# Row maximum of the softmax over the state subtracted by GpSimd in five of eight batches, with another order of operations

## The chip, the cores and the metric

The kernel runs on one core of a Trainium2 chip. Its time is the device time of one execution in microseconds (us); times of several executions are given as a median. Engines are called TensorE (PE in the profile), VectorE (DVE), ScalarE (ACT), GpSimd (POOL) and SyncE (SP, which only issues transfers here).

## The reference, cut to what matters

Two stages. The first is an attention between x (8 batches, 8 heads, 512 rows, 64 columns) and a state (8, 8, 32 rows, 64 columns), with a softmax in each direction. The second runs over the 544 rows of both results, 512 columns wide (all heads), with a convolution of three rows between two products.

```python
def _attn_ref(x, state):                      # x: 8,8,512,64   state: 8,8,32,64
    scores = scale * np.matmul(x, state.transpose(0, 1, 3, 2))
    scores = scores - scores.max(-1, keepdims=True)      # over the 32 rows of the state
    a = np.exp(scores)
    a /= a.sum(-1, keepdims=True) + 1e-09
    xread = np.matmul(a, state)
    scores2 = scale * np.matmul(state, x.transpose(0, 1, 3, 2))
    ...                                                  # the same softmax, over the 512 rows of x
    return np.concatenate([xread, np.matmul(a2, x)], axis=2)

def _moe_ref(x, w_in, conv_w, w_out):         # x: 8,544,512   w_in: 512,1024   w_out: 1024,512
    h = np.maximum(x @ w_in, 0.0)
    conv_out = ...                            # conv_w[0]*row before + conv_w[1]*row + conv_w[2]*row after
    gate = 1.0 / (1.0 + np.exp(-conv_out))
    return h * gate @ w_out
```

## The kernel before

Nothing is looped at run time: the program is one straight list of 1,673 operations, made in a fixed numbering and then put out in the order that the string ORDER gives. Each engine runs its own operations in that order, and waits only where data or a buffer asks for it. A number in ORDER is an operation; a negative number -n puts n blocks of filler products on TensorE; a `v` behind a number runs an operation that is ScalarE's on VectorE. BANKS gives, in the same order, which of eight PSUM banks each result takes. Transfers are issued from SyncE's queue in the list's order too, so a load that waits for a free buffer holds those behind it.

For each batch b the steps are these.

- `xt_load`, `x_load`: x is loaded twice, transposed (tag `xt`, four buffers) and plain (tag `xx`).
- `scores` (TensorE) and `keep_scores`: the scores of both directions, kept in a buffer `at` of 128x1024.
- `top`, `exp2`, `norm2`, then `flip` or `turn`, `read`, `divide`, `read_flip`: the softmax over x and its product, for the 32 state rows.
- `softmax(b)`, for batches 1 to 7: the softmax over the 32 rows of the state, in ten operations on a buffer `af` of 128x1024, of which there is one. `att_flip` (L477, VectorE) transposes blocks of 32, `att_top` (L481, VectorE) takes the maximum of each 32, `att_sub` (L484) subtracts it, `att_exp` (L487, ScalarE), `att_sum` (L491, VectorE), `att_norm`, `att_div` (L498), `att_back` (L501), all VectorE, then the split into a rounded part and a rest, `att_high` (ScalarE) and `att_low` (VectorE). Batch 0 has a softmax of its own in halves.
- `state_product(b, hf)` (L588): the state times a half of w_in, so that the read of x and its product with w_in become one product; the result is split into two parts as well (`state_high`, `state_low`). Its two buffers have the tags `u0` and `u1`, two buffers each, or those that ELSEWHERE names.
- `hidden`, for steps i = 8 b + f with f from 0 to 7: six products (L677) from the split scores and the split state product, then `relu` (L216, ScalarE mostly), `join` and `edge` (L695: copies of one element per partition, on ScalarE for batches 0 to 2 and on GpSimd from batch 3), `middle`, two taps `before` (L720) and `behind` (L725), `sigmoid` (L729), `gate` (L734), the split `gate_high` (L221) and `gate_low` (L224), and twelve products `project` (L752) with w_out.

Weights are loaded in pieces and rounded by ScalarE and VectorE (`w_abs` to `w_sign`) at the start. Every large product from batch 1 on is made three times, with the high and low parts (PASSES). The 64 rows of both sides at the ends of the batches go through the smaller operations `side_...` and `tail`.

Of the kernel before, what the change touches and what calls it, by code (L numbers as in the profile page):

```python
# [13 lines left out]
ALU = mybir.AluOpType  # L14
# [37 lines left out]
ELSEWHERE = {(B - 1, 0): "xt", (B - 1, 1): "xt", (B - 2, 1): "at"}  # L52
# [12 lines left out]
01234567012342147536047260413756043175231253540504646457065407654075647040601324576723015145145720  # L65
1364527301037010143640171657632323420232402476371654207654120721740521640450740156052404370334063
# [3 lines left out]
99 0 -1 122 -5 -7 -1 -1 -1 -1 -1 -1 -1 100 102 121 1 125 127v 21 101 126 103 104 22 24 128 143 144 151 129 23 25 15 17  # L70
# [3 lines left out]
208 541 159 55 137 138 526 500 209 517 502 479 480 528v 481 56 210 163 164 165 211 63 65 213 529 569 570 518 242 599  # L74
# [35 lines left out]
1567 1129 1124 1557 1565 1130 1568 1133 1163 1134v 1137v 1125 1569 1148 1164 1167 379 1131v 1570 1149 1152 1138 1135  # L110
1139 1140 1165 1168 1153 422 1141 380 381 382 417 1150 1571 1178 1142 1166 1136 383 1154 1143 1179 1572 1238 1182 1169
1155 1156 420 421 1574 418 419 1193 1194 1157 416 1208 1196 1170 1195 1171 1239 1241 1181 1223 1146 425 1197v 426 1172
1158 1183 1261 1306 1209 1210 1180 1211 423 1151 424 1224 1198 1291 1184 1185 1145 1160 1147 1186 1240 1262 1199 1161
1265v 1173 1263 1200 1201 1187 1144 1188 1266 1267 1212 1264 1268 1213 1214 1321 1269 1575 1307 1202 1576 1308 1322
1324 1226 1323 1175 1227v 1159 1174 1162 1177 1215 1216 1176 1203 1573 1228 1577 1578 1242 1243 1579 1225 1229 1244
1192 1230 1231 1207 1190 1217 1205 1232 1245 1246 1276 1325 1126 1191 1206 1189 1277 1204 1292 1366 1218 1580 1294
1219 458 459 1221 1582 1583 1278 1279 1367 1369 1233 1247 1248 1310 1311 1222 1295 1309 1584 1585 1586 1236 1270 1220
1370 1251 1257v 460 1293 463 465 1271 464 1280 1258 468 1234 466 1587 1296 1297 1237 1252 1312 461 1235 1298 1259 1260
1588 1313 1368 1595 1249 1281 1253 462 1326 1581 1299 1389 1273 1282 1283 1284 1285 1596 1254 1351 1352 1390v 1391
1250 1300 1392 1314 1589 1255 1275 1336 1371 1337 469 1327 1132 1286 1301 1597 1598 1274 1289 1599 1272 1419 1434 1288  # L120
1303 1315 1316 1340 1339 1328 1329 1330 1318 1420 1423 1590 1593 1592 1393v 1331 1304 1290 1305 1600 1355v 1356 1422
1353 1338 1372 467 1479 1357 1404 1341 1342 1358 1601 1394 1333 1373 1374 1343 1344 1603 1287 1302 1317 1435 1405 1407
1436 1602 1604 1605 1606 1332 1359 1320 1360 1361 1607 1608 1421 1408v 1609 1335 1319 1424 1464 1406 1425 1345 1375
1395 1396 1449 1346 1350 1376 1611 1348 1334 1349 1364 1347 1362 1612 1613 1409 1363 1438v 1437 1410 1411 1377 1614
# [48 lines left out]
def fused_kernel(ctx: ExitStack, tc: tile.TileContext, xT, xn, stT, w_in, conv_w, w_out, out):  # L173
# [62 lines left out]
    add = plan.add  # L236
# [229 lines left out]
    def rows(b):  # L466
        return af[b].rearrange("p (k n) -> p k n", n=NS)
# [4 lines left out]
    def per_row(t):  # L472
        return t.unsqueeze(2).broadcast_to([P, KT, NS])
# [9 lines left out]
    def att_sub(b):  # L483
        V.tensor_tensor(rows(b), rows(b), per_row(s1.pop(b)), op=ALU.subtract)  # L484
# [529 lines left out]
```

## Time and profile before

| | |
|---|---|
| median of 2 executions | 354.12 us (354.07 to 354.16) |
| the profiled execution | 353.49 us |
| its span, first to last instruction | 351.7 us |
| TensorE, VectorE, ScalarE, GpSimd busy | 344.9, 317.1, 255.1, 29.0 us |
| products on TensorE (as recorded) | 2505 |
| bytes moved | 39.24 MB |

The span is what the trace covers; the time of an execution has about 1.8 us around it. The views show times from the span's start.

### The profile page before, as it was taken

Reading aid. Unit: us, or ns where it says so; the run is one execution under the profiler, and the core shown is the slowest. Engines: PE = TensorE matmul, PEld = TensorE weight load, DVE = VectorE, ACT = ScalarE, POOL = GpSimd, SP = SyncE. Lnnn points to the kernel's source line nnn. Section 1 sums busy time; section 2 is a strip of 40 time slices with the busy share of each in tenths; the row PEclk is TensorE's granted clock in tenths of the full one; section 3 lists DMA queues with packets and bytes.
Section 4 is the critical chain, followed back from the end, with each engine's and each line's share of the span. In section 5 each row is a group of like instructions: output and inputs, shape, how many; then the busy total and the mean of one; then the engine's idle time right before and its main releaser. Section 6 shows DMA issues by size and latency. Waiting matters only on the chain.

```text
span 351.7 us, 6630 instructions
## 1 busy us (share of the span) xinstructions
PE 344.9 (98%) x2505; PEld 269.0 (76%) x2505; DVE 317.1 (90%) x545; ACT 255.1 (73%) x554; POOL 29.0 (8%) x90
## 2 busy tenths in 40 slices
PE   8998999999999999999999999999999999999995
PEld 5765767788688877887788878886887678888884
DVE  1999999999999999999999999989997898899870
ACT  2998999998778888786975677647766865564462
POOL 1000000000000000030110112000411101122000
PEclk9999999999999999999999999999999999999999
DMA  7999988323730255152110010010000021001024
GB/s 237 389 337 361 331 292 332 123 66 104 253 121 0 69 174 178 63 178 79 43 60 2 0 60 33 30 60 32 2 2 0 30 91 31 22 3 37 0 89 149
DMA packets 19343, 39.24 MB, mean 112 GB/s; under 512 B 1904, under 2 KB 8176, under 8 KB 19312
## 3 DMA queue, kind: packets, MB, share of 16 engines
q1 hardware_dynamic: 18880, 38.54, 31.6%
q8 instruction: 19, 0.31, 0.4%
q10 hardware_dynamic: 432, 0.29, 0.3%
q14 instruction: 12, 0.10, 0.1%
HBM read 27.81 MB, written 11.01 MB: 110 GB/s over the span
## 4 chain that ended last, share of the span: by engine, by line
PE 95%; DMA 3%; DVE 1%; issue 0%; ACT 0%
PE acc L752 47%; PE ps_h L677 22%; PE ps_hs L662 4%; PE ps_u L595 4%; PE acc_t L752 3%; DMA xt<-xT 3%; PE ps_h L684 3%; PE ps_r L401 2%; PE ps_s L325 2%; PE idle L233 2%; PE acc_c L752 2%; PE acc L766 2%; PE ps_t L372 1%; PE ps_x L542 1%; PE ps_f L414 0%; DVE nm L354 0%
## 5 line engine op out<-in xcount | busy, mean ns | idle before, releaser
L752 PE MATMUL acc<-wo,g 128*128 128x512 f32 x723 | 175.6, 393 | 0.0
L752 PEld LDWEIGHTS acc<-wo,g 128*128 128x128 f32 x723 | 134.6, 188 | 29.3 <-issue 1.3
L677 PE MATMUL ps_h<-a,u 128*128 128x512 f32 x336 | 82.8, 392 | 0.1
L677 PEld LDWEIGHTS ps_h<-a,u 128*128 128x128 f32 x336 | 62.5, 188 | 14.1 <-ACT u L221 0.8
L729 ACT ACTIVATE t<-t 128x512 f32<-128x512 f32 x64 | 40.0, 630 | 19.5 <-DVE t L725 19.4
L725 DVE SCALAR_TENSOR_TENSOR t<-h,cw,t 128x512 f32<-128x512 f32 (+1 forms) x64 | 47.0, 745 | 0.7
L720 DVE SCALAR_TENSOR_TENSOR t<-h,cw,t 128x511 f32<-128x511 f32 x64 | 46.9, 744 | 0.4 <-ACT t L210 0.3
L221 ACT ACTIVATE g<-t 128x512 fp32r<-128x512 f32 (+1 forms) x62 | 38.3, 621 | 12.3 <-DVE t L734 8.8
L734 DVE SCALAR_TENSOR_TENSOR t<-t,h 128x512 f32<-128x512 f32 (+1 forms) x64 | 42.2, 668 | 4.1 <-ACT t L729 4.0
L224 DVE TENSOR_TENSOR g<-t,g 128x512 fp32r<-128x512 f32 (+1 forms) x62 | 41.2, 673 | 3.4 <-ACT g L221 3.3
L216 ACT ACTIVATE h<-ps_h 128x512 f32<-128x512 f32 x59 | 34.8, 599 | 11.7 <-PE ps_h L677 8.3
L210 ACT ACTIVATE t<-h,cw 128x512 f32<-128x512 f32 x53 | 38.0, 725 | 0.7 <-DVE g L224 0.5
L695 POOL COPY h<-hs 128x1 f32<-128x1 f32 x40 | 15.3, 400 | 136.7 <-DVE t L734 111.8
L772 ACT ACTIVATE o<-acc 128x512 f32<-128x512 f32 (+1 forms) x30 | 16.2, 554 | 10.8 <-PE acc L752 7.4
L695 POOL COPY hs<-h 128x1 f32<-128x1 f32 x40 | 13.3, 349 | 83.9 <-ACT h L216 69.8
L224 DVE TENSOR_TENSOR u<-ps_u,u 128x512 fp32r<-128x512 f32 x28 | 18.7, 682 | 0.7 <-ACT u L221 0.7
L662 PEld LDWEIGHTS ps_hs<-sr,wi 128*128 128x128 f32 x128 | 16.2, 191 | 2.8 <-ACT at L210 0.8
L662 PE MATMUL ps_hs<-sr,wi 128*128 128x128 f32 x128 | 16.8, 277 | 0.0
L221 ACT ACTIVATE u<-ps_u 128x512 fp32r<-128x512 f32 x28 | 16.1, 598 | 0.6 <-PE ps_u L595 0.6
L261 ACT ACTIVATE hc<-raw 128x512 f32<-128x512 f32 (+1 forms) x17 | 11.4, 673 | 5.7 <-DMA raw<-w_in 3.0
L684 PE MATMUL ps_h<-p,u 128*128 128x256 f32 x64 | 14.8, 384 | 0.0
L684 PEld LDWEIGHTS ps_h<-p,u 128*128 128x128 f32 x64 | 11.8, 190 | 3.3 <-ACT u L210 0.8
(103 smaller groups left out, 388.0 us busy)
## 6 DMA issues: line engine op xcount, KB each, us to landing
xt<-xT SPq DMA_DIRECT2D x16, 512.0 KB, 7.5
xx<-xn SPq DMA_DIRECT2D x16, 512.0 KB, 5.9
out<-o SPq DMA_DIRECT2D x27, 256.0 KB, 2.1
raw<-w_in SPq DMA_DIRECT2D x8, 512.0 KB, 7.5
raw<-w_out SPq DMA_DIRECT2D x8, 512.0 KB, 8.2
far<-tv SPq DMA_DIRECT2D x8, 256.0 KB, 2.1
e2t<-far SPq DMA_DIRECT2D x8, 256.0 KB, 2.8
out<-o SPq DMA_DIRECT2D x6, 128.0 KB, 1.7
```

The source lines that it names most:

```text
L210: A.activation(dst, src, AF.Copy, scale=scale)
L216: A.activation(dst, src, AF.Relu, scale=0.5)
L221: A.activation(hi, src, AF.Copy)
L224: engine.tensor_tensor(lo, src, hi.bitcast(F32), op=ALU.subtract)
L662: PE.matmul(ps_hs[m, f][:, :NT], wi[:, k, f * P:(f + 1) * P], sr[m][:, k, :], start=(k == 0), stop=(k == NK - 1))
L677: PE.matmul(ps_h[i], u[j][:, g, fs], a[k][:, g, :], start=(n == 0), stop=(n == 3 * NG - 1))
L684: PE.matmul(ps_h[f][:, q * HS:(q + 1) * HS], us[0, f // 4][0][:, g, f % 4 * P:(f % 4 + 1) * P], half_of(pa[0], q)[:, g, :], start=(g == 0) ...
L720: V.scalar_tensor_tensor(t[:, 1:], h[:, :S - 1], cw[:, f, 0:1], t[:, 1:], op0=ALU.mult, op1=ALU.add)
L725: V.scalar_tensor_tensor(t[:, :n], h[:, 1:n + 1], cw[:, f, 2:3], t[:, :n], op0=ALU.mult, op1=ALU.add)
L729: A.activation(tt[i], tt[i], AF.Tanh, scale=0.25)
L734: V.scalar_tensor_tensor(tt[i][:, :n], tt[i][:, :n], 1.0, hd[i][:, :n], op0=ALU.add, op1=ALU.mult)
L752: PE.matmul(acc, g[j][:, cs], wo[:, k, f, :], start=(f == 0 and n == 0), stop=(f == end and n == 2))
```

## The change

`att_sub` of batches 3 to 7 runs on GpSimd. Of the state products, the second halves of batches 3 to 7 take buffers of tag `xt` and the first half of batch 7 takes `at`; before, both halves of batch 7 took `xt` and the second half of batch 6 took `at`. ORDER and BANKS are others throughout; the operations and their dependencies are the same. The list has the same 14 filler calls at its start.

```diff
+SHARED = (3, 4, 5, 6, 7)
+
-ELSEWHERE = {(B - 1, 0): "xt", (B - 1, 1): "xt", (B - 2, 1): "at"}
+ELSEWHERE = {**{(b, 1): "xt" for b in range(3, B)}, (B - 1, 0): "at"}
...
-99 0 -1 122 -5 -7 -1 -1 -1 -1 -1 -1 -1 100 102 121 1 125 127v 21 101 126 103 104 22 24 128 143 144 151 129 23 25 15 17
+0 121 -1 -5 -7 122 -1 -1 -1 -1 99 100 102 101 103 104 1 125 127 126 128 143 144 129 151 15 16 21 152 22 24 -1 -1 -1 23
...
     def att_sub(b):
-        V.tensor_tensor(rows(b), rows(b), per_row(s1.pop(b)), op=ALU.subtract)
+        (G if b in SHARED else V).tensor_tensor(rows(b), rows(b), per_row(s1.pop(b)), op=ALU.subtract)
...
-        add("DVE", "wide", partial(att_sub, b), r=[m], w=[f])
+        add(*(("POOL", "broad") if b in SHARED else ("DVE", "wide")), partial(att_sub, b), r=[m], w=[f])
```

Written out by name, the new list has this on VectorE (V) and GpSimd (G) from the maximum to the row sum of a batch, other engines left out:

```
batch 3: V att_top, before 17, behind 16, behind 17 | G att_sub | V gate 16, gate 17, turn, before 18, gate_low 16 | V att_sum
batch 4: V att_top, behind 24, before 25, gate 26, side_tap, before 28 | G joins 29, 31, att_sub | V side_tap, gate 24, behind 25, behind 28, G edge 25 | V att_sum
batch 7: V att_top, ... | G join 35 | V ..., side_low | G att_sub | V gate_low 29, gate_low 28, gate 30, side_tap, behind 31, G join 33 | V att_sum
batch 6: V att_top | G edges 33, 34, 38 | V side_tap, gate_low 33, side_tap, gate 32, G edge 32 | G att_sub | V gate 35, gate_low 32, gate_low 34, G joins 37, 39 | V att_sum
batch 5: V att_top, gate 38, gate_low 37 | G att_sub | V gate_low 38, side_tap, gate_low 39 | V att_sum
```

Transfers at the start, in the order of SyncE's queue, up to the xT load that the scores of batch 1 need last (w: a piece of weights, st: state; 512 KB each, but st0 64 KB, st1 448 KB; a small one on ScalarE's queue is left out):

```
before: xt1 xt0 st0 w3 w2 w1 w0 st1 w5 w4 w6 xt5 xt4 w7 x(0,0) w8 x(0,1) xt3 xt2
after:  xt0 xt1 st0 w2 w3 w5 w0 w1 w4 xt4 w6 st1 xt5 w8 w7 x(0,0) w9 x(0,1) xt2 xt3
```

## Rows read from the trace of the kernel before

**Rows 1.** The page: busy us and instructions by engine; shares of the chain.
```profile
PE 344.9 (98%) x2505; PEld 269.0 (76%) x2505; DVE 317.1 (90%) x545; ACT 255.1 (73%) x554; POOL 29.0 (8%) x90
...
PE 95%; DMA 3%; DVE 1%; issue 0%; ACT 0%
```

**Rows 2.** Stretches: us; busy by engine (count), from PE to POOL; PEclk, DMA share, GB/s.
```profile
10.00:30.00 20.00, 19.72 (x349) 14.62 (x348) 19.90 (x41) 19.61 (x45) 0.00 (x0) 1.00 0.99 349
35.00:340.00 305.00, 304.90 (x2030) 240.59 (x2029) 287.71 (x482) 225.03 (x487) 27.67 (x82) 1.00 0.25 86
50.00:200.00 150.00, 150.00 (x1151) 119.18 (x1150) 148.24 (x239) 120.87 (x277) 7.84 (x27) 1.00 0.34 113
200.00:340.00 140.00, 139.90 (x688) 111.20 (x688) 125.34 (x222) 89.50 (x177) 19.83 (x55) 1.00 0.09 32
```

**Rows 3.** The chain in order of time: start us, us, what.
```profile
1.03 6.41 PE idle L233 x24
...
8.49 0.40 DVE at L212
...
12.19 0.61 DVE m L536
...
22.82 9.15 DMA xt<-xT
...
33.19 1.02 PE ps_t L372 x8
...
77.49 0.68 PE acc L752 x3
```

**Rows 4.** Waits of PE's products: us in total, times, longest.
```profile
PE ps_s L325 <- DMA xt<-xT: 1.6, 1, 1.6
...
PE acc L757 <- ACT o L772: 0.5, 1, 0.5
```

**Rows 5.** Groups by line and shape: busy us, mean ns | idle before.
```profile
L720 DVE SCALAR_TENSOR_TENSOR t<-h,cw,t 128x511 f32<-128x511 f32 x64 | 46.9, 744 | 0.4 <-ACT t L210 0.3
...
L224 DVE TENSOR_TENSOR g<-t,g 128x512 fp32r<-128x512 f32 x56 | 37.9, 686 | 3.4 <-ACT g L221 3.3
...
L802 DVE SCALAR_TENSOR_TENSOR ss<-hs,cw,ss 128x128 f32<-128x128 f32 x32 | 11.0, 344 | 2.1 <-ACT ss L798 1.0 <-POOL hs L695 0.7
...
L484 DVE TENSOR_TENSOR af<-af,m 128x1024 f32<-128x1024 f32 x7 | 8.6, 1222 | 0.0
...
L487 ACT ACTIVATE af<-af 128x1024 f32<-128x1024 f32 x7 | 7.4, 1058 | 4.7 <-DVE af L484 4.7
...
L380 DVE STREAM_TRANSPOSE tv<-e 128x512 f32<-128x512 f32 x8 | 5.5, 701 | 0.6 <-ACT e L363 0.5
```

**Rows 6.** Groups by line and shape, GpSimd alone.
```profile
L695 POOL COPY h<-hs 128x1 f32<-128x1 f32 x40 | 15.3, 400 | 136.7 <-DVE t L734 111.8 <-ACT hs L666 16.5 <-issue 8.3
...
L198 POOL TENSOR_SCALAR eight<-ident 128x128 f32<-128x128 f32 x1 | 0.5, 532 | 0.1
...
masks.py:199 POOL TENSOR_SCALAR_AFFINE_SELECT ident<-ident 128x128 f32<-128x128 f32 x1 | 0.3, 292 | 0.0
```

**Rows 7.** Timeline, 154.4 to 157.6 us, VectorE and GpSimd: start us, us, what.
```profile
154.47 0.69 DVE L224 TENSOR_TENSOR g<-t,g 128x512 fp32r<-128x512 f32 x1
154.65 0.56 POOL L695 COPY hs<-h 128x1 f32<-128x1 f32 x1 [12.45 <-ACT h L216]
...
156.88 0.71 DVE L380 STREAM_TRANSPOSE tv<-e 128x512 f32<-128x512 f32 x1
156.95 0.18 POOL L695 COPY hs<-h 128x1 f32<-128x1 f32 x1
```

**Rows 8.** Timeline: batch 5's last split and its first hidden product.
```profile
234.63 1.21 DVE L224 TENSOR_TENSOR a<-at,a 128x1024 fp32r<-128x1024 f32 x1
...
236.44 1.75 PE L677 MATMUL ps_h<-a,u 128*128 128x512 f32 x7
```

**Rows 9.** Issues of xT: ns min/median/max; first and last start in us.
```profile
L312 SPq DMA_DIRECT2D xt<-xT x16: 327/420/1251, 0.7 to 86.0; - x16
```

More of the change, by code (lines that the diff above doesn't have):

```diff
@@ L64 @@
 BANKS = """
-01234567012342147536047260413756043175231253540504646457065407654075647040601324576723015145145720
-1364527301037010143640171657632323420232402476371654207654120721740521640450740156052404370334063
+01234567012345143726027604537264027135270357125425142514652415421261524615613710265307126466242514
+6375321064106101561075450575462412431314036125461275306473506140763701050704577054651633023704215
 """
 ORDER = """
-99 0 -1 122 -5 -7 -1 -1 -1 -1 -1 -1 -1 100 102 121 1 125 127v 21 101 126 103 104 22 24 128 143 144 151 129 23 25 15 17
[3 rows of a table removed]
@@ L74 @@
-208 541 159 55 137 138 526 500 209 517 502 479 480 528v 481 56 210 163 164 165 211 63 65 213 529 569 570 518 242 599
[35 rows of a table removed]
[L110 to L123, printed above, removed]
@@ L124 @@
-1395 1396 1449 1346 1350 1376 1611 1348 1334 1349 1364 1347 1362 1612 1613 1409 1363 1438v 1437 1410 1411 1377 1614
-1354 1365 1380 1379 1450v 1453 1397 1398 1412 1610 1615 1494 1480v 1616 1617 1399 1401 1618 1256 1454 1594 1451 1465
-1413 1452 1439 1440 1619 1620 1403 1621 1426 1387 1388 1441 1467 1455 1442 1622 1443 1414 1427 1378 1456 1623 1624
-1402 1481 1482 1495v 1625 1498v 1416 1428 1457 1483v 1499 1591 1429 1418 1400 1415 1497 1433 1635 1636 1637 1638 1639
[3 rows of a table removed]
-1514 1516v 1656 1517 1493 1509 1650 1657 1658 1659 1524v 1490 1505 1462 1510 1508 1512 1525 1663 1511 1513 1477 1492
@@ L132 @@
-1520 1515 1662 1660 1522v 1523 1521 1661 1507 1518 1519
[3 rows of a table added]
+45 191 475 474 525 123 31 193 57 192 205 206 526 32 207 194 46 48 47 528v 49 52 54 511 512 498 499 540 513 50 208 529
[36 rows of a table added]
+1561 1149 1151 379 1562 1152 1134 1135 1179 1563 1131v 380 1150 1153 1154 417 1155 1132 382 422 420 423 418 1564 1137v
+381 1125 1138 1182 383 1156 1113 1139 1140 1565 419 421 1163 1164 1165 1181 1193 1157 1194v 1141 1197v 1238 1566 1306
+1291 1167 1136 424 1142 1168 1169 1166 1208 425 1143 1195 1145 1196 1083 1180 1209 1292 1158 1198 1567 1568 1199 1144
@@ new lines @@
+1159 1170 1171 1200 1201 1239 1294 1242 1295 1241 1183 1243 1128 1160 1261 1223 1224 1184 1146 1161 1240 1244 426 1172
+1173 1185 1186 1245 1187 1126 1276 1227v 1277v 1174 1147 1162 1226 1188 1212v 1213 1177 1246 1210 1211 1569 1192 1176
+1228 1225 458 1189 1570 1214 1202 1571 1191 1203 1175 1215 1278 1262 1264 1572 1229 1230 1247 1190 1206 1574 1216 1217
+1231 1321 1263 1248 1218 1351 1221 1296 1232 1322v 1233 1293 1307 1310 1311 1297 1575 1324 1204 1265 1266 1267 1576
+1577 1578 1579 1236 1207 1222 1268 459 1298 1237 1252 1269 1251 1205 1220 1280 1580 465 1309 1259v 1352 1355v 460 1281
@@ new lines @@
+1260 466 1353 1282 1323 463 464 1235 461 1573 467 1581 1250 462 1434 468 1356 1270 1404 1308 1312 1219 1313 1582 1357
+1271 1283 1284 1389 469 1299 1285 1583 1584 1279 1585 1255v 1256 1586 1587 1464 1234 1249 1336 1286 1588 1589 1314
+1390 1358 1359 1325 1273 1257v 1393 1394 1300 1301 1275 1290 1337v 1338 1392 1274 1315 1595 1253v 1254 1258 1316 1354
+1596 1597 1598 1326 1340v 1327 1288 1366 1599 1303 1367v 1391 1289 1304 1405v 1600 1601 1328 1329 1603 1408 1341 1604
+1419 1590 1342 1343 1407 1395 1449 1591 1605 1606 1607 1608 1609 1272 1420v 1344 1287 1421 1422 1594 1360 1302 1305
[3 rows of a table added]
@@ new lines @@
+1426 1641 1618 1362 1377 1468v 1469 1619 1620 1380 1381 1382 1470 1451 1621 1363 1622 1439 1623 1436 1440 1624 1625
+1402 1364 1627 1427 1417 1453v 1428 1378 1383 1480 1481 1403 1387v 1388 1495 1496 1401 1441 1416 1628 1629 1630 1429
+1431 1483 1626 1454 1455 1456 1471 1442 1484 1379 1384 1631 1482 1632 1457 1633 1472 1400 1385 1485 1415 1386 1443
+1430 1498v 1444 1486 1643 1644 1645 1487 1418 1473 1433 1634 1646 1458 1432 1446 1459 1474 1488 1489 1647 1648 1447
+1649 1651 1461 1652 1497 1653 1642 1499 1654 1655 1656 1500 1476 1491 1445 1460 1501 1650 1657 1658 1659 1662 1502
@@ L133 @@
+1663 1661 1448 1463 1475 1490 1660 1478 1493 1503 1504 1506 1514v 1515 1509 1524v 1525 1505 1510v 1512v 1516 1511 1513
+1462 1508 1477 1492 1520 1522v 1523 1507 1517 1521 1518 1519
 """
```

82 rows, old and new, of the table ORDER are left out of this document.

## The prediction

> **What bounds the kernel now.** I read the views in this order. First the page's busy times [rows 1]: TensorE is busy 98% of the span, VectorE 90%, ScalarE 73%, GpSimd 8%. A share of the whole says little, so next the stretches [rows 2]: from 35 to 340 us TensorE is busy for 304.90 of 305 us, at a granted clock of 1.00, its higher level of 2.4 GHz. The reader is to see that VectorE runs beside it almost without a pause from 50 to 200 us (148.24 of 150) and gets air only later (125.34 of 140). Then the chain that ended last: 95% TensorE, 3% transfers, 1% VectorE [rows 1]. In order of time [rows 3] it shows where something else than useful products is on it: fillers of 6.41 us until the first loads have landed at 7.44 us; VectorE steps of the first softmax, nine pieces that begin at 8.49 and end at 12.80 us; a transfer of xT that lands at 31.96 us. TensorE's own waits [rows 4] are few: 1.6 us for that transfer, 0.5 us for an evacuation at the end.
>
> So TensorE's sequence of products is the time, and the change neither adds nor removes a product; the 14 filler calls are the same too. **What could be won is bounded**: the VectorE pieces cover at most 12.80 - 8.49 = 4.3 us, the waits 1.6 and 0.5 us, 6.4 us in all if everything vanished. Two per cent of 354.12 is 7.1 us (about what a measurement of this kernel can tell from no change). The fillers end when the first state and xT loads land, and the new list needs these first as well.
>
> **The subtraction.** Five of seven VectorE instructions of 1.222 us leave (L484) [rows 5]: 6.1 us less on VectorE. GpSimd gets five of the same shape, 128x1024 from two SBUF inputs, which no row shows. The nearest rows are GpSimd's own [rows 6]: a 128x128 scaling takes 532 ns, a 128x128 select 292 ns, a one-element copy with nothing in its way 0.18 us [rows 7]. With 0.18 us as the fixed part, an element per partition costs (532 - 180)/128 = 2.75 ns or (292 - 180)/128 = 0.88 ns, so 1024 cost 3.0 us or 1.1 us with the fixed part. I take 3.0, from the scaling, which like the subtraction streams and computes; 1.1 stays the lower end. The Trainium skill, GPSIMD Engine Reference, 3.1 Elementwise, states that a two-input operation takes 1.96 times VectorE's time there; an estimate by it is 1.96 x 1.222 = 2.4 us, which no run here shows, and by it the loss summed below would be 4.4 us and not 7.3.
>
> **Where it lands.** The subtraction waits for VectorE's maximum (L481), and ScalarE's exponential for GpSimd. Behind the subtraction GpSimd has only one-element copies (the edge of step 25 in batch 4; joins 37, 39, 38 in batch 6; 33 and 32 in batch 7), whose readers are VectorE's second taps. Behind the exponential ScalarE has relus, gate splits and divides; it is 73% busy and can catch up. VectorE's next step of the chain is the row sum. Until then the new list gives VectorE other work, which I priced by its rows [rows 5]: 3.5 us in batch 3 (two gates and a gate split of 0.69, a turn of 0.70, a tap of 0.74), 2.5 in batch 4, 1.7 in batch 5, 2.1 in batch 6, 3.1 in batch 7. Subtraction and exponential (1.06 us) take 4.06 us. So VectorE stands for 0.6 + 1.5 + 2.3 + 2.0 + 0.9 = 7.3 us in all, in the place of the 6.1 us of which it is relieved. With the lower end (2.16 us together) it stands for 0.5 us, in batches 5 and 6. Besides, GpSimd's copies wait for VectorE: their mean is 400 ns [rows 6] against 180 with nothing in the way, 0.2 us each, 1.0 us for five subtractions. Sum: 8.3 us.
>
> **How late VectorE may be.** I went through both order lists and added up each engine's operations at the means of their rows (most of them in [rows 5]), less the 0.07 us by which successive VectorE operations overlap, and three products as 0.68 us [rows 3]. At the first hidden product of batch 5, VectorE's list up to that batch's last split is 9.8 us longer than TensorE's list in the kernel before, and there the product starts at 236.44, 0.60 us after the split's end at 235.84 [rows 8]. In the new list it is 3.0 us longer: 6.8 us more room, 5.8 of them the five subtractions, which all stand ahead of this place. So VectorE may lose 6.8 + 0.6 = 7.4 us before TensorE waits there. In batches 3 and 4 the room grows by 0.6 and 2.9 us, for one and two subtractions, and is not used up. The loss of 8.3 us exceeds the room by 0.9 us: **+0.9 us**. By the lower end (1.5 us) nothing is left over. Without this cover each microsecond of VectorE would cost one, as TensorE has no pause later in which to make it up [rows 2].
>
> **State products in buffers of xT and scores.** No instruction is added. The second halves of batches 3 to 7 take two of four xT buffers each. The last transfer into those is issued at 86.0 us [rows 9], and the new list has all sixteen far ahead of the first such product, so none is blocked. What is freed is the pair of u buffers, and among TensorE's waits [rows 4] no product stands for one. Zero.
>
> **Another order, at the start.** Up to the last block of the first batch's state product, just ahead of the scores that wait for the transfer, both lists hold the same products in another sequence. Then the new list has two groups of transposes ahead of these scores: 8 products of 1.02 us [rows 3], of which 0.9 fall into the wait of 1.6 us. That is -0.9 us if the transfer lands as before. Against it, 512 KB more are queued ahead of the transfer (9,752 against 9,240 KB, added up from the list); at the 349 GB/s of 10 to 30 us [rows 2] that is 1.5 us, +0.6 net. The transfer may also be issued earlier, since fewer loads that wait for a buffer stand ahead of it on SyncE's queue. I take the middle, **-0.2 us**, with -0.9 and +0.6 as ends. SyncE's other moved loads and stores lie beside a TensorE that is full.
>
> **The end.** The last products, the evacuation between them and the last store stand in the same sequence in both lists, and the new one has more TensorE work ahead of its last gate split. Zero; at best 0.5 us.
>
> **Sum.** The profiled execution took 353.49 us, 1.79 around a span of 351.70, and lies 0.63 below the median. 353.49 + 0.9 - 0.2 = 354.2 us; carried to the median, 354.8.
>
> **Rivals.**
>
> *A shared way into SBUF.* The rows show GpSimd giving way [rows 7]: a copy that takes 0.18 us beside a transpose takes 0.56 us beside a tensor-tensor operation, and ends 0.05 us after it. The VectorE operation keeps its 0.69 us. That speaks against a cost to VectorE, but a copy is too short to show one. If a subtraction that has begun holds VectorE's next two-input operation until it ends, VectorE loses its whole duration, and in the new list such an operation (a gate, a tap, a gate split) stands right behind each of the five. Five times 1.1 is 5.5 us, inside the room of 7.4; five times 3.0 is 15.0, 7.6 us over it. It decides from 1.5 us each. Time 353.9 (the sum without the 0.9) to 361.5; I take the middle, 357.7. This is the case that ends slower. The Trainium skill, SBUF — State Buffer, Who interferes with whom, states that such a pair contends and that whoever is first blocks the other for the whole instruction; with 2.4 us each it would be 4.6 us over the room. The trace agrees with one half of it, the copies that wait.
>
> *The start goes worse.* If the weights of that last block come late by one more load, 1.5 us on top of the +0.6, everything behind moves: 354.8 + 0.2 + 0.6 + 1.5 = 357.1 us. Against it: ahead of that block VectorE and ScalarE have the same work in both lists (23.1 against 24.1, and 23.2 against 23.4 us).
>
> *The start goes better, and nothing is lost later.* If half of the 6.4 us bound went: 354.1 - 3.2 = 350.9 us. For it speaks that VectorE has 1.0 us less ahead of the block; against it, that both engines are busy for 19.90 and 19.61 of 20 us there [rows 2].
>
> **How the numbers follow.** Forecast 354.8 us with chance 0.53, its own range 353.0 (no loss, and the start at -0.9) to 356.0. The shared way 0.31, the worse start 0.11, the better start 0.05. The range reaches into the shared way and the worse start until 2 in 10 are left out: 352.6 to 358.7. Faster than -2% (below 347.0) lies beyond the bound above: 0.01. Slower than +2% (above 361.2) needs the top of the shared way, or it and the worse start: 0.06. The rest, 0.93, is within.
>
> **What would show it.** TensorE without idle time from 35 to 340 us; VectorE some 6 us less busy, with L720, L725, L734 and L224 as long as before. Under the shared way these rows' means grow, with single operations over 2 us beside the subtraction, and TensorE waits for splits in batches 4 to 6. GpSimd's new row should read 1 to 3 us. Well above 3 us would make the prediction wrong, as would a TensorE wait longer than 1.6 us before 35 us.

## The result

The changed kernel takes 357.89 us (two executions, 357.75 and 358.03) against 354.12 us: ratio 1.0107, 95% interval 1.0063 to 1.015, within the 2% that a measurement can tell, but above 1. Beside other kernels, and compared with the kernel before on the same chip each time, it gave 1.006 [1.004, 1.0081] and 1.0085 [1.0062, 1.0107]. So it is slower by 0.6 to 1.1%, 2 to 4 us. The forecast was 354.8 us; the time is that of the rival with the shared way into SBUF (357.7 us).

The page of the changed kernel, with the lines that answer to [rows 1] and the new group of GpSimd (line numbers are 2 higher than before):

```profile
PE 349.0 (98%) x2505; PEld 268.2 (75%) x2505; DVE 323.4 (91%) x545; ACT 252.7 (71%) x549; POOL 43.4 (12%) x95
...
PE 66%; DVE 19%; ACT 4%; DMA 3%; issue 3%; SPq 0%; DVEq 0%
...
L486 POOL TENSOR_TENSOR af<-af,m 128x1024 f32<-128x1024 f32 x5 | 11.9, 2376 | 55.2 <-DVE m L483 55.2
```

Five subtractions have left VectorE, 6.1 us of work, and it is busy for 6.3 us more than before, not less (3.1 of them come with the new list: with all subtractions on VectorE, e1 below, it is busy for 320.2 us; the new list has 28 operations with a `v`, which VectorE runs in ScalarE's place, the list before 22). The chain that ended last holds 19% VectorE in place of 1%. The span is 356.2 us, the granted clock 0.998 over the run. The long stretch of [rows 2], from PE to POOL:

```profile
35.00:340.00 305.00, 304.16 (x2022) 236.70 (x2015) 293.48 (x484) 223.18 (x483) 42.10 (x87) 1.00 0.26 88
```

From 35 to 340 us TensorE is idle for 0.84 of 305 us, before for 0.10. So most of the loss of 3.8 us doesn't show as idle time (the ends of products are modelled, so that one which starts late mostly makes the one ahead of it look longer). TensorE's waits, answering to [rows 4], are no longer than before either:

```profile
PE ps_u L597 <- DMA st<-stT: 1.1, 1, 1.1
...
PE acc L759 <- ACT o L774: 0.5, 1, 0.5
PE acc L754 <- DVE g L226: 0.3, 1, 0.3
```

VectorE's groups by line and shape, answering to [rows 5] (taps, gate splits and gates), and behind them the two lines of before that [rows 5] leaves out.

```profile
L722 DVE SCALAR_TENSOR_TENSOR t<-h,cw,t 128x511 f32<-128x511 f32 x64 | 47.1, 739 | 1.7 <-ACT t L212 1.6
L727 DVE SCALAR_TENSOR_TENSOR t<-h,cw,t 128x512 f32<-128x512 f32 x56 | 42.7, 773 | 0.7 <-DVE ss L811 0.3
L226 DVE TENSOR_TENSOR g<-t,g 128x512 fp32r<-128x512 f32 x56 | 40.7, 737 | 3.8 <-ACT g L223 3.5
L736 DVE SCALAR_TENSOR_TENSOR t<-t,h 128x512 f32<-128x512 f32 x56 | 39.4, 712 | 1.5 <-ACT t L731 1.4
```

```profile
L725 DVE SCALAR_TENSOR_TENSOR t<-h,cw,t 128x512 f32<-128x512 f32 x56 | 41.0, 745 | 0.7
L734 DVE SCALAR_TENSOR_TENSOR t<-t,h 128x512 f32<-128x512 f32 x56 | 37.8, 685 | 4.1 <-ACT t L729 4.0
```

Gate splits have gone from a mean of 686 ns to 737, which over 56 is 2.9 us, second taps from 745 to 773 and gates from 685 to 712. A mean hides how that comes about; the timeline of the changed kernel around batch 4's subtraction shows it (GpSimd first, then VectorE):

```profile
164.18 2.43 POOL L486 TENSOR_TENSOR af<-af,m 128x1024 f32<-128x1024 f32 x1
...
164.10 0.74 DVE L722 SCALAR_TENSOR_TENSOR t<-h,cw,t 128x511 f32<-128x511 f32 x1
164.76 2.00 DVE L804 SCALAR_TENSOR_TENSOR ss<-hs,cw,ss 128x128 f32<-128x128 f32 x1
166.69 0.68 DVE L736 SCALAR_TENSOR_TENSOR t<-t,h 128x512 f32<-128x512 f32 x1
```

The tap of 128x128 takes 2.00 us where its group before has a mean of 344 ns, and ends 0.15 us behind the subtraction. There is one such operation at each of the five subtractions, none elsewhere: a tap at 124.42 us (1.66 us longer than usual), the one at 164.76 (1.66), a gate at 184.71 (1.72), gate splits at 212.42 (1.68) and 230.46 (1.46). Together 8.2 us, which is more than the 6.1 us saved. The held operation is not always the first one behind the recorded start of the subtraction. In batch 5 a gate split that began 0.44 us behind it kept its 0.68 us, and the next one was held:

```profile
229.16 2.90 POOL L486 TENSOR_TENSOR af<-af,m 128x1024 f32<-128x1024 f32 x1 [10.16 <-DVE m L483]
...
229.60 0.68 DVE L226 TENSOR_TENSOR g<-t,g 128x512 fp32r<-128x512 f32 x1
230.46 2.15 DVE L226 TENSOR_TENSOR g<-t,g 128x512 fp32r<-128x512 f32 x1 [0.18 <-ACT g L223]
```

So the recorded start alone doesn't tell which of the two engines had the way.

### The profile page after: what moved, and what is told of

It reads as the page before. It is cut to its first block, busy times and chain, and to the rows that moved or that the text cites. A ratio compares the mean times of both kernels' runs of the same rounds, so it can differ in the third digit from the quotient of the medians.

```text
span 356.2 us, 6644 instructions
## 1 busy us (share of the span) xinstructions
PE 349.0 (98%) x2505; PEld 268.2 (75%) x2505; DVE 323.4 (91%) x545; ACT 252.7 (71%) x549; POOL 43.4 (12%) x95
## 4 chain that ended last, share of the span: by engine, by line
PE 66%; DVE 19%; ACT 4%; DMA 3%; issue 3%; SPq 0%; DVEq 0%
PE acc L754 32%; PE ps_h L679 17%; PE ps_hs L664 3%; DMA xx<-xn 3%; DVE g L226 3%; PE acc_t L754 3%; DVE t L727 3%; PE ps_u L597 2%; PE ps_h L686 2%; DVE t L722 2%; PE ps_r L403 2%; DVE t L736 2%; PE acc_c L754 2%; PE acc L768 2%; PE ps_s L327 1%
## 5 line engine op out<-in xcount | busy, mean ns | idle before, releaser
L727 DVE SCALAR_TENSOR_TENSOR t<-h,cw,t 128x512 f32<-128x512 f32 (+1 forms) x64 | 48.6, 769 | 0.7 <-DVE ss L811 0.3
L226 DVE TENSOR_TENSOR g<-t,g 128x512 fp32r<-128x512 f32 (+1 forms) x62 | 43.9, 718 | 3.8 <-ACT g L223 3.5
L736 DVE SCALAR_TENSOR_TENSOR t<-t,h 128x512 f32<-128x512 f32 (+1 forms) x64 | 43.7, 692 | 1.6 <-ACT t L731 1.4
L218 ACT ACTIVATE h<-ps_h 128x512 f32<-128x512 f32 x57 | 33.7, 600 | 10.6 <-PE ps_h L679 8.7
L212 ACT ACTIVATE t<-h,cw 128x512 f32<-128x512 f32 x54 | 39.0, 729 | 0.3
L697 POOL COPY hs<-h 128x1 f32<-128x1 f32 x40 | 19.2, 493 | 93.2 <-ACT h L218 78.1
L774 ACT ACTIVATE o<-acc 128x512 f32<-128x512 f32 (+1 forms) x24 | 13.5, 569 | 12.6 <-PE acc L754 4.1
L697 POOL COPY h<-hs 128x1 f32<-128x1 f32 x40 | 12.0, 313 | 60.1 <-DVE t L736 49.0
L486 POOL TENSOR_TENSOR af<-af,m 128x1024 f32<-128x1024 f32 x5 | 11.9, 2376 | 55.2 <-DVE m L483 55.2
L597 PE MATMUL ps_u<-wi,st 64*32 64x512 f32 x224 | 14.1, 597 | 1.1 <-DMA st<-stT 1.1
```

The source lines that it names most:

```text
L212: A.activation(dst, src, AF.Copy, scale=scale)
L218: A.activation(dst, src, AF.Relu, scale=0.5)
L226: engine.tensor_tensor(lo, src, hi.bitcast(F32), op=ALU.subtract)
L697: G.tensor_copy(dst, src)
L727: V.scalar_tensor_tensor(t[:, :n], h[:, 1:n + 1], cw[:, f, 2:3], t[:, :n], op0=ALU.mult, op1=ALU.add)
L736: V.scalar_tensor_tensor(tt[i][:, :n], tt[i][:, :n], 1.0, hd[i][:, :n], op0=ALU.add, op1=ALU.mult)
```

## The experiments

The theory after the result: a GpSimd subtraction that has the way holds VectorE's next operation with two SBUF inputs until it ends. Its rivals: the new order and buffers cost the time; or the softmax's way from VectorE over GpSimd to ScalarE has become too long, without any hold.

Besides the ratio, each kernel has one number from its own trace. TensorE runs the 24 products of the last steps' shares (`acc_c`) once, at 87 to 91 us, and three products of 128x256 at the very end. **From the start of the one to the start of the other** the kernels with the new list do the same products in the same order, and so do, among themselves, those with the list before; how well the first loads fell doesn't enter. For the changed kernel (its run c1) and the same with all subtractions on VectorE (e1), the timeline has:

```profile
88.30 5.60 PE L754 MATMUL acc_c<-wo,last 128*128 128x512 f32 x24
...
350.66 0.62 PE L759 MATMUL acc<-wo,g 128*128 128x256 f32 x3 [0.47 <-ACT o L774]
```

```profile
89.24 5.60 PE L754 MATMUL acc_c<-wo,last 128*128 128x512 f32 x24
...
348.52 0.62 PE L759 MATMUL acc<-wo,g 128*128 128x256 f32 x3 [0.47 <-ACT o L774]
```

350.66 - 88.30 = 262.36 us against 348.52 - 89.24 = 259.28 us. All kernels, with this stretch; a ratio is to the kernel before on the same chip in the same set, where it took 354.1 to 354.8 us:

| kernel | list | median us | ratio to before [95%] | stretch us |
|---|---|---|---|---|
| before | old | 354.12 | 1 | 260.42 |
| e4, idle memsets | old | 355.10 | 1.0017 [0.9991, 1.0043] | 260.48 |
| e5, idle copies | old | 355.19 | 1.0017 [0.9988, 1.0046] | 260.79 |
| e2, subtraction on GpSimd | old | 356.76 | 1.0071 [1.0046, 1.0096] | 262.26 |
| e3, idle subtractions | old | 359.11 | 1.0123 [1.0065, 1.0182] | 264.36 |
| e1 and e10, all on VectorE | new | 353.84, 353.99 | 0.9983 [0.9958, 1.0009], 0.9996 [0.9972, 1.0019] | 259.28, 259.24 |
| e7, batch 3 alone, covered | new | 354.67 | 1.0008 [0.9988, 1.0028] | 259.86 |
| e6 and e9, memsets in its place | new | 354.92, 355.47 | 1.0009 [0.9978, 1.004], 1.004 [1.002, 1.0061] | 260.93, 260.98 |
| the change | new | 357.89 | 1.0107 [1.0063, 1.015] | 262.47 |
| c1 and c2, the change again | new | 357.0, 357.38 | 1.006 [1.004, 1.0081], 1.0085 [1.0062, 1.0107] | 262.36, 262.48 |
| e8, in four pieces | new | 359.56 | 1.0134 [1.0097, 1.0171] | 265.54 |

Where a kernel was run twice, the stretch repeats within 0.12 us.

**e1: the new list and buffers, without GpSimd.**

```diff
-SHARED = (3, 4, 5, 6, 7)
+SHARED = ()
```

> The changed kernel with its own list and buffers, but all subtractions back on VectorE. If a running GpSimd subtraction holds VectorE's next two-input operation (shared way), the five operations that read 2.0 to 2.4 us instead of 0.3 to 0.7 are normal again, VectorE is 2.1 us less busy (5 x 1.222 back, 8.2 of stretching gone), and most of the 2.9 us that TensorE loses between 120 and 260 us comes back, not the 1.7 us lost before: 355.0 to 356.4 us. If the list itself is to blame, nothing changes but VectorE's 6.1 us more: 357.5 us or more.

No VectorE operation is stretched, and the time is that of the kernel before and below the 355.0 to 356.4 us expected. The order and the buffers, taken by themselves, cost nothing that can be measured; what the change costs is in the subtraction's move. A second set, of five rounds, gave the same:

> The new list and buffers with all subtractions on VectorE again, in five rounds. The kernel with memsets in their place stands between this one (0.9983) and the changed kernel. If the handing over costs nothing: ratio 1.001 to 1.003, as with the memsets. If it costs about as much as the hold: 0.996 to 1.000, and TensorE loses as little after 100 us as in the kernel before.

Its 0.9996 lies with the second case, that the handing over costs as well, but its interval reaches into the first; the stretch decides that below (e6).

**e2: the list and buffers of before, the subtraction on GpSimd.**

```diff
+SHARED = (3, 4, 5, 6, 7)
...
-        V.tensor_tensor(rows(b), rows(b), per_row(s1.pop(b)), op=ALU.subtract)
+        (G if b in SHARED else V).tensor_tensor(rows(b), rows(b), per_row(s1.pop(b)), op=ALU.subtract)
```

> The kernel before with its own list and buffers, the subtraction of batches 3 to 7 on GpSimd. Shared way: five VectorE operations stretched by 1.5 to 1.7 us each, net 2.1 us more on VectorE, in a list that leaves it 0.6 us of room at batch 5: 356 to 359 us. If the list is to blame: 354.1, within 0.6 us. If only the later hand-over costs (subtraction 2.4 instead of 1.2 us, exponential right behind): VectorE's row sum waits up to 1.5 us per batch, no operation is stretched, 355 to 358.

Five operations are stretched by 1.66 to 1.73 us, 8.5 us together, and the stretch grows by 262.26 - 260.42 = 1.8 us. The move costs in either list.

**e3: the kernel before, and five more subtractions on GpSimd that nobody waits for.** They work on a buffer that is no longer used, at the places where batches 3 to 7 subtract; VectorE keeps its own.

```diff
     def att_sub(b):
+        if b in SHARED:
+            G.tensor_tensor(spare(), spare(), per_row(zeros[:, :KT]), op=ALU.subtract)
         V.tensor_tensor(rows(b), rows(b), per_row(s1.pop(b)), op=ALU.subtract)
```

> The kernel before, complete on VectorE, with five extra GpSimd subtractions of the same shape on a buffer that nobody needs any more (the last rows' gate, minus zeros), one at the place of each subtraction of batches 3 to 7. Nobody waits for them. Shared way: five VectorE operations are stretched by some 1.6 us, 8.2 us more on VectorE without any relief, so 358 to 362 us. Later hand-over or list: 354.1, within 0.6 us.

```profile
89.86 2.96 POOL L490 TENSOR_TENSOR last<-last,zeros 128x1024 f32<-128x1024 f32 x1 [10.14 <-DVE last L226]
...
90.36 0.68 DVE L741 SCALAR_TENSOR_TENSOR t<-t,h 128x512 f32<-128x512 f32 x1
90.96 2.41 DVE L727 SCALAR_TENSOR_TENSOR t<-h,cw,t 128x511 f32<-128x511 f32 x1
```

An operation without any reader stretches a VectorE tap from 0.74 to 2.41 us. Five stretches of 0.70 to 1.72 us, 6.1 together, lengthen TensorE's stretch by 264.36 - 260.42 = 3.9 us. That is the hold, shown without any longer chain. The two small ones (0.70 us) are subtractions of which the first 1.1 us ran beside a transpose.

**e4: the same places, two memsets instead**: GpSimd only writes.

```diff
+        if b in SHARED:
+            G.memset(last, 0.0)
+            G.memset(last, 0.0)
```

> As the one with five extra subtractions, but with two memsets of 128x1024 at each place, which write and read nothing. If only GpSimd's reads share a way with VectorE's second input: no VectorE operation is stretched, 354.1 us within 0.6. If any long GpSimd operation holds VectorE: stretched operations again, as long as the memsets, and 356 us or more.

```profile
157.09 0.95 POOL L490 MEMSET last<- 128x1024 f32 x1
...
157.54 0.31 DVE L810 SCALAR_TENSOR_TENSOR ss<-hs,cw,ss 128x128 f32<-128x128 f32 x1
```

Ten memsets, 954 and 956 ns in the mean, no VectorE operation stretched, a stretch of 260.48 us. The time of 355.10 us lies above what was expected, but the kernel before took 354.39 us in that set, and the ratio can't be told from 1. That GpSimd is busy with writes costs nothing here.

**e5: the same places, a copy**: one SBUF input instead of two.

```diff
+        if b in SHARED:
+            G.tensor_copy(spare(), spare())
```

> The kernel before, and at the five places where batches 3 to 7 subtract GpSimd copies an idle SBUF buffer of 128x1024 onto itself: one SBUF input, nobody waits for it. If any long GpSimd operation that reads SBUF holds VectorE: five stretched VectorE operations, 356 to 359 us as with the idle subtraction (359.1). If only one with two SBUF inputs does: none is stretched, 354.4 to 355.1 us as with the idle memsets.

```profile
157.04 1.04 POOL L490 COPY last<-last 128x1024 f32<-128x1024 f32 x1
...
156.86 0.70 DVE L382 STREAM_TRANSPOSE tv<-e 128x512 f32<-128x512 f32 x1
157.49 0.74 DVE L809 SCALAR_TENSOR_TENSOR ss<-hs,cw,ss 128x128 f32<-128x128 f32 x1
```

Neither expectation fits whole. A copy holds VectorE too: this tap takes 0.74 us instead of 0.35, and two more operations lengthen by 0.78 and 0.58 us. But four of the five copies take only 1.04 us (the first, which had to wait, 2.11), in two places the copy stood beside transposes for most of that, and the five cost some 1.8 us of VectorE and 0.4 us of TensorE, which the ratio can't tell from none.

**e6 and e9: the changed kernel with memsets in the subtractions' place.** The subtraction of batches 3 to 7 is left out; GpSimd writes the same buffer for 2.4 us instead, and ScalarE waits for it as in the change.

```diff
-        (G if b in SHARED else V).tensor_tensor(rows(b), rows(b), per_row(s1.pop(b)), op=ALU.subtract)
+        if b in SHARED:
+            s1.pop(b)
+            G.memset(af[b], 0.0)
+            G.memset(af[b], 0.0)
+            G.memset(af[b][:, :NG * S // 2], 0.0)
+        else:
+            V.tensor_tensor(rows(b), rows(b), per_row(s1.pop(b)), op=ALU.subtract)
```

> The changed kernel, but in batches 3 to 7 GpSimd's subtraction is left out and two and a half memsets of the same buffer, 2.4 us together, stand in its place (the attention weights of these batches come out equal for every column). VectorE is relieved as in the change, and the softmax waits for GpSimd as long as in the change; only the reading of two SBUF inputs is gone. Shared way (GpSimd's reads hold VectorE): no stretched VectorE operation, 353.8 us as with the subtraction on VectorE (352.8 to 354.8). Rival, that the handing over from VectorE to GpSimd to ScalarE costs the time: 357.9 us as in the change.

> The kernel with memsets in the subtractions' place again, beside the changed kernel on the same chip, in more rounds, since the intervals of the two touched at 1.004. Shared way: ratio 0.998 to 1.002, no stretched operation. Handing over: the changed kernel's ratio.

The timeline of e6 around batch 4, GpSimd and then VectorE, and from its table of VectorE's waits the row of the row sum:

```profile
161.74 0.95 POOL L488 MEMSET af<- 128x1024 f32 x1
162.75 0.95 POOL L489 MEMSET af<- 128x1024 f32 x1
163.76 0.53 POOL L490 MEMSET af<- 128x512 f32 x1
...
162.33 0.35 DVE L810 SCALAR_TENSOR_TENSOR ss<-hs,cw,ss 128x128 f32<-128x128 f32 x1
...
165.41 1.22 DVE L499 TENSOR_REDUCE s<-af 128x32 f32<-128x1024 f32 x1 [0.59 <-ACT af L495]
```

```profile
DVE s L499 <- ACT af L495: 4.0, 3, 2.3
```

The tap that took 2.00 us in the change takes 0.35. But the kernel doesn't fall back to the time with everything on VectorE. VectorE now stands 4.0 us, in three of five batches, until the exponential is done; neither the change (where VectorE is itself held while the chain runs) nor e1 has this row. The stretch parts the cost: 260.95 - 259.26 = **1.7 us for the longer way** over GpSimd, and 262.44 - 260.95 = **1.5 us for the hold** (means of the rows in the table). The memsets with the gaps between them take 2.55 us and the subtraction 2.38 in the mean, so the first part is rather too large and the second too small; and the parts hold for this order, the hold taken out while the longer way stays. Against the kernel before the two ratios of this kernel leave -0.2 to 0.6%, so by ratios alone the first part would not be certain. The second shows in them, if barely: 1.004 [1.002, 1.0061] against 1.0085 [1.0062, 1.0107] on one chip, 1.0009 [0.9978, 1.004] against 1.006 [1.004, 1.0081] on another. Both theories were right in part.

Why the longer way costs anything, although VectorE has 6.1 us less to do, shows at batch 5, the place that the prediction worked out. The last split of this batch and its first hidden product, in e1 and then in e6:

```profile
235.09 1.23 DVE L226 TENSOR_TENSOR a<-at,a 128x1024 fp32r<-128x1024 f32 x1 [0.43 <-ACT a L223]
...
236.72 0.39 PE L679 MATMUL ps_h<-a,u 128*128 128x512 f32 x1
```

```profile
236.23 1.23 DVE L226 TENSOR_TENSOR a<-at,a 128x1024 fp32r<-128x1024 f32 x1
...
237.23 0.78 PE L685 MATMUL ps_h<-a,u 128*128 128x512 f32 x2
```

In e1 the product starts 0.40 us after the split's end at 236.32. In e6 the split ends at 237.46, 0.23 us after the first product has started, and the next two start 0.17 us late. Counted from `acc_c` (89.24 us in e1, 88.63 in e6), VectorE ends this split 1.75 us later in e6 than in e1. On the way there it is idle for 9.0 of 148.8 us, in e1 for 2.7 of 147.1: 4.0 us of it are the waits for the exponential, 4.2 those for other results of ScalarE. What VectorE was relieved of did not become a lead.

**e8: each subtraction in four pieces of 128x256.**

```diff
+        m, n = s1.pop(b), 4 if b in SHARED else 1
+        for k in range(n):
+            ks = slice(k * KT // n, (k + 1) * KT // n)
+            (G if n > 1 else V).tensor_tensor(rows(b)[:, ks, :], rows(b)[:, ks, :],
+                                              m[:, ks].unsqueeze(2).broadcast_to([P, KT // n, NS]), op=ALU.subtract)
```

> The changed kernel, with each of GpSimd's five subtractions in four pieces of 128x256, about 0.65 us each. If the hold lasts as long as one GpSimd instruction: no VectorE operation is stretched by more than 0.7 us, but several behind each other can be, and pieces that find a VectorE operation running wait for it; the sum of the stretches is at most that of the change (8.2 us), the time 354.5 to 357.9 us. If what counts is that GpSimd is busy, however it is cut: operations stretched by 1.5 us and more as before, 358 us or, with the added fixed parts, 359.

```profile
161.44 3.80 POOL L489 TENSOR_TENSOR af<-af,m 128x256 f32<-128x256 f32 x4
...
162.02 0.70 DVE L808 SCALAR_TENSOR_TENSOR ss<-hs,cw,ss 128x128 f32<-128x128 f32 x1
162.65 1.10 DVE L740 SCALAR_TENSOR_TENSOR t<-t,h 128x512 f32<-128x512 f32 x1
163.68 2.12 DVE L731 SCALAR_TENSOR_TENSOR t<-h,cw,t 128x512 f32<-128x512 f32 x2
```

The hold is one instruction long, as expected: a tap that took 2.00 us takes 0.70, no operation lengthens by more than 0.43 us, and the two engines take turns. The time was not expected. GpSimd waits in its turn for each VectorE operation, so the four pieces take 3.80 us instead of 2.43; the exponential comes later by that, VectorE stands for it at three row sums (4.3 us; 4.0 in e6), and TensorE's stretch is 3.1 us longer than in the change. A shorter hold for VectorE was paid with a longer chain.

**e7: batch 3 alone on GpSimd, with three transposes behind it** in VectorE's list; batches 4 to 7 on VectorE.

```diff
-SHARED = (3, 4, 5, 6, 7)
+SHARED = (3,)
...
-att_top 3, before 17, behind 16, behind 17, att_sub 3, gate 16
+att_top 3, att_sub 3, turn 15, turn 14, turn 12, before 17, behind 16, behind 17, gate 16
```

(The second part is written out by the names of the operations; transfers that follow the moved transposes moved with them.)

> The changed kernel with only batch 3's subtraction on GpSimd (batches 4 to 7 on VectorE), put right behind the maximum, and three VectorE transposes of 128x512 (steps 15, 14 and 12, 0.70 us each) moved right behind it, so that they run beside it; the second tap that stood there comes after them. If only VectorE operations with two SBUF inputs are held: the transposes that begin after the subtraction keep 0.70 us, the tap behind them is stretched by at most 0.3 us, and the time is that with the subtraction on VectorE, ratio 0.998 to 1.001. If any VectorE operation that begins beside a subtraction is held: the first transpose behind it takes over 2 us. Rival for the time: steps 14 and 15 come 8 us later than before, and a read waits for them: 355 to 356 us.

```profile
121.63 1.92 POOL L494 TENSOR_TENSOR af<-af,m 128x1024 f32<-128x1024 f32 x1 [43.24 <-DVE m L491]
...
121.39 1.29 DVE L390 STREAM_TRANSPOSE tv<-e 128x512 f32<-128x512 f32 x2
122.98 0.71 DVE L390 STREAM_TRANSPOSE tv<-e 128x512 f32<-128x512 f32 x1 [0.29 <-ACT e L373]
123.61 0.73 DVE L730 SCALAR_TENSOR_TENSOR t<-h,cw,t 128x511 f32<-128x511 f32 x1
```

Two transposes begin after the subtraction and keep their 0.7 us, and the tap behind it keeps its 0.73. The subtraction, with nothing to wait for, takes 1.92 us. So here, at one subtraction, the hold was scheduled away. It is no gain over e1 all the same: 0.6 us longer in the stretch, and in the ratio no difference.

## Why the prediction was right or wrong

- **The number.** 357.89 us lies in the range of 352.6 to 358.7 us only because that had been widened over the rival; the forecast's own range ended at 356.0. (Its lower end, no loss and the start at -0.9 us, adds up to 353.2 and not 353.0.)
- **Bound on the gain, order, buffers, start:** right as far as the ratios can tell. With the subtraction left on VectorE they are 0.9983 and 0.9996, each known to some 0.25% or 0.9 us; the forecast had -0.2 us for the start and zero for the buffers. That VectorE would be some 6 us less busy was wrong even without any hold: in e6 it is busy for 315.7 us, 1.4 less than before; the new list has six operations more that VectorE runs in ScalarE's place. In the changed kernel's first profile the start waited 1.1 us for a state transfer in place of the 1.6 us for xT, and in the second for no transfer at all.
- **The end:** right; the wait of 0.5 us for the evacuation is unchanged.
- **The subtraction's price:** 3.0 us was taken between 1.1 and 3.0; measured, 2.38 us as a mean in the change, of which 1.92 is the operation with nothing in its way (e7) and the rest is waiting for the VectorE operation that was already running. The estimate from the Trainium skill, GPSIMD Engine Reference, 3.1 Elementwise, was 2.4 us; the trace agrees with it in the change, but alone the operation takes 1.92 / 1.222 = 1.57 times VectorE's time, not 1.96.
- **Where it lands:** right in kind. Without the hold VectorE stands 4.0 us for the exponential; the sum said 7.3 us with 3.0 us each.
- **How late VectorE may be, the step that failed: the term of +0.9 us.** It measured 262.44 - 259.26 = 3.2 us. Two things were wrong in it. First, the room of 7.4 us did not exist. By the step's own figures 7.4 - 5.8 = 1.6 us of it should be there with all subtractions on VectorE, and 7.4 - 4.0 = 3.4 us be left in e6; at the product that was worked out, e1 has 0.40 us, and in e6 the split comes 0.23 us after the product's start. The relief was counted as a lead, but VectorE spent it waiting for ScalarE. Nor was one place an allowance for the whole run. Set beside e1, product by product from `acc_c` on, TensorE in e6 falls behind by 0.6 us at 166 to 168 us, 0.3 at 213, 0.2 at 228, 0.2 at 238 (the place worked out) and 0.4 from 325 to 340 us. In the change it falls behind, besides, where e6 loses nothing: by 0.9 us at 134 to 139 us, behind batch 3's hold of 1.66 us, where the step had found 0.6 us of added room, and by 0.6 us at 188 us, behind the gate held at 184.71. Secondly, the hold was in none of its terms: "L720, L725, L734 and L224 as long as before" is what the traces contradict.
- **The rival that came true.** That a subtraction once begun holds VectorE's next two-input operation is shown by e3 against e4 (with and without reading, nobody waiting) and by e6 against the change. The Trainium skill, SBUF — State Buffer, Who interferes with whom, says it: such a pair contends, a GpSimd instruction that only writes does not, and whoever is first has the way for the whole instruction. Every run here agrees. Its time of 357.7 us was hit, its working only in part, and so the hit is in part luck. The holds were 8.2 us in five, which against a room of 7.4 would have cost 0.8; that the time came out in the middle of the rival's range is because the room did not exist, and the longer way cost 1.7 us besides.
- **The copies of [rows 7]** were read as evidence against a cost to VectorE. They showed half the rule: VectorE was first there, and GpSimd gave way.

It stays open which part of the 1.7 us of the longer way is the added 1.2 us per batch of GpSimd's work and which the handing over between three engines; no run parts them.

## What to carry to other kernels

Moving an elementwise operation from VectorE to GpSimd relieved VectorE here only where what stood next in its list could run beside it. Look for VectorE operations with two SBUF inputs right behind, add for each moved operation what is left of it when the next of them begins, and compare with what is saved; here 8.2 us were held for 6.1 us saved. Transposes could be put beside it (e7), but cutting it into pieces only traded the hold for a longer chain (e8). And where one engine has no idle time at all, check the room for a delay at each of its inputs, not at one, and don't count work taken off another engine as a lead while that engine waits for a third.

## What the runs showed of the hardware

- A one-input copy on GpSimd holds VectorE too: a tap of 0.35 us took 0.74 beside a copy of 1.04 us (e5). A memset of the same size (0.95 us) does not (e4, e6).
- The hold works both ways, by the instruction: subtractions cut into four alternate with VectorE's operations (0.70 and 1.10 us instead of 0.35 and 0.68), and the four take 3.80 us (e8).
- VectorE transposes that begin during a GpSimd subtraction are not held (0.7 us), nor do they delay it (1.92 us) (e7).
